# Attention and a mixture of experts on one core: four shared PSUM places, another order of a pair's jobs, the sums' guard on VectorE, own orders for the last pairs and the first expert block

## The chip, the core and the metric

The kernel runs on one core of a Trainium2 chip. The core has five engines with a queue each, worked off in order: TensorE (PE in the profile, with PEld for its weight loads), VectorE (DVE), ScalarE (ACT), GpSimd (POOL) and SyncE (SP, which here only issues DMAs). Matmul results go to PSUM, which is eight banks of 2 KB in each of 128 partitions; a tile of 128x512 fp32 numbers is one bank. The metric is the device time of one execution in microseconds (us), as the median of several runs.

## What is computed

Attention over 8 batches, 8 heads, 576 tokens of 64 numbers, and then a mixture of 8 experts, one for each token, over the 4608 rows that attention leaves.

```python
q_rot, k_rot = (rotate(q), rotate(k))
scores = scale * np.matmul(q_rot, k_rot.transpose(0, 1, 3, 2))
attn = np.exp(scores - np.max(scores, axis=-1, keepdims=True))
attn = attn / (np.sum(attn, axis=-1, keepdims=True) + 1e-09)
x = np.matmul(attn, v)            # to rows: 4608 x 512
logits = x @ w_gate + modality_bias[modality_id]
e_idx = np.argmax(logits, axis=1) # gate_w: the softmax at e_idx
h = np.maximum(x[mask] @ w1[e], 0.0)           # for each expert e
out[mask] = gate_w[mask, None] * (h @ w2[e])   # 512 -> 1024 -> 512
```

## The kernel before

**A pair's jobs.** Attention goes by 32 pairs of heads (`n`, four to a batch). Each pair is cut into named jobs, and each job is a call that puts its instructions on one engine:

- `T1`, `T2`, `R`, `HI`, `LO`, `SWH`, `SWL` rotate q and k two pairs ahead (POOL, and ACT for HI), split them into a high and a low part in a tile HL, and copy them by DMA to SW with the heads' halves of the partitions exchanged.
- `S0` to `S8` (`scores`, L314) are the scores of nine sets of 128 queries, six matmuls each (S8 twelve). `MN` (`rowmin`, L323, DVE) takes the extreme of a row, `EX` (`expo`, L330, ACT) the exponential with the row's sum.
- `F0` to `F3`, `FA`, `FB` (`fill`, L336, PE) transpose the exponentials into PSUM, 16 transposes to a full fill. `A_F` and `B_F` (`evac`) bring the two banks back to SBUF tiles PH and PD, one on ACT (L274), one on DVE (L368).
- `AVA` and `AVB` (`AV`, L392) multiply with V, `OTA` and `OTB` copy the result to SBUF (ACT), `OUT` (`outp`, L422) turns it and multiplies with the gate's weights, `EVA` and `EVB` (`ev`, DVE, three instructions each) divide by the row sums. For that `RE` (L406, ACT) adds 1e-9 to the sums and `RI` (L409, DVE) takes the reciprocal.
- Every fourth pair ends a batch: `XO` writes its rows to the DRAM tensor X, and fifteen steps of `route` on all engines, with five scatters `SC` (L532, POOL), put the batch's tokens into the experts' table TAB.

**PSUM.** S and F take the next of three places of two banks in turn (`RING`, `ring()`); AV, OUT and the routing's count take tiles of one bank from a pool of two (`psA`).

**The order.** No engine's order comes from a scheduler. Each job has a key (`KEYS`) in us; job x of pair n is sorted by `KEYS[x] + 14.438 * n`, and every engine gets its jobs in that order. A table `AT` has keys for the rest. Pairs 0, 1, 30 and 31 have some keys of their own.

**The experts.** The rows are worked through in blocks of 256 for one expert. A block (`s`) needs eight gathers of 128x128 numbers from X on POOL (`m_gather`, L795, 4 for each half of its rows) into one of two tiles XG (even blocks the one, odd blocks the other); DVE transposes both halves (`m_tr`, L840); ACT and DVE split them into XTH and XTL (`m_tre`). ACT and DVE split the weights into W1H, W1L, W2H and W2L (`m_hi`, `m_lo`). PE then runs four parts of the first layer (`l1.0` to `l1.3`, `m_l1`, L860, 24 matmuls each), ACT and DVE apply relu and split (`m_l1e`, L869 and L870), and PE runs the second layer for two halves of the rows (`m_l2`, L883, 24 matmuls each). ACT scales the result (L886), and POOL scatters it (L888).

The first block's work and the gathers of the first three blocks are jobs among the last pairs'. Block 1's gathers carry a wait for a matmul of block 0's first layer, the one that was last issued when the gather is written (`after`). From the second block on the code is a plain loop (`chain`), in whose order block 1's transposes and splits come first on DVE and ACT, ahead of block 0's results.

Of the kernel before, what the change touches and what calls it, by code (L numbers as in the profile page):

```python
# [8 lines left out]
F32 = mybir.dt.float32  # L9
# [36 lines left out]
AT = dict(
    rk=(23.0, 28.55, 31.2, 36.9, 41.45, 43.0, 44.4, 45.7, 54.6, 56.9, 57.4, 58.85, 60.2, 70.35, 73.3),
    bias=15.6,
    sc=(73.4, 87.85, 102.3, 116.7, 116.75),
    sce=(73.4, 73.45, 87.85, 87.9, 102.3),  # L50
    pl=(58.9, 70.4, 73.35, 84.85, 87.75, 99.3, 102.2, 113.7, 116.6),
    plan=(-49.7, -35.2, 6.0, 9.0),
    ix=(-41.5, -3.9, 6.1, 9.1),
    sine=-48.9,
    rows=(((0, -27.5, None), (1, -13.05, None), (2, -12.4, None), (3, -2.9, (30, "av", 0)), (5, 0.45, (30, "av", 1)),
           (7, 4.75, (30, "out", 1))), ((0, 11.15, ("l1", 0)),), ((0, 16.5, None),)),
    w1=(-21.6, -21.5, -16.2, -16.1),
    w2=(-9.9, -9.8, -9.7, -9.6),
    hi=(-14.8, -14.7, -0.4, -0.3),
    lo=(-11.8, -1.6, 10.8, 10.85),  # L60
    tr=(10.2, 10.21),
    te=(10.3, 10.4),
    hi2=(10.5, 10.98, 11.1, 11.2),
    lo2=(11.5, 11.55, 11.65, 11.75),
# [1141 lines left out]
```

## Time and profile before

| | us |
|---|---|
| median of 3 runs | 936.58 |
| lowest and highest | 933.55, 946.05 |
| the profiled execution's own time | 934.42 |
| its span from the first to the last instruction | 932.6 |
| granted TensorE clock over the span | 0.996 |

The profile gives one execution. Times in its views are us from the start of the span, durations of one instruction are in us in the timeline and in ns in the groups. A matmul's start is measured and its end modelled, so that overlapping matmuls count as busy also where they wait for each other. The pairs run from some 32 to 490 us, the expert blocks from 495 us to the end.

### The profile page before, as it was taken

What the parts mean: (1) busy time and instruction counts of PE and PEld (TensorE: products, weight loads), DVE (VectorE), ACT (ScalarE), POOL (GpSimd) and SP (SyncE); (2) the same over time, 40 slices, a digit from 0 to 9 for tenths busy, and PEclk for the clock granted to TensorE, in tenths of its full rate; (3) what the DMA queues carried; (4) which work ended last, traced back from release to release, by engine and by line L of the source; (5) the groups of instructions that cost most, each with busy time, mean ns of one, the idle gap of its engine ahead of it and who ended that gap; (6) DMA issues with size and microseconds to landing.
All of it is one profiled execution on the core that took longest, in us unless ns stands there. A gap on an engine that the chain in (4) does not pass through costs nothing.

```text
span 932.6 us, 24974 instructions
## 1 busy us (share of the span) xinstructions
PE 894.4 (96%) x9248; PEld 738.7 (79%) x9248; DVE 682.6 (73%) x1221; ACT 623.0 (67%) x1291; POOL 659.1 (71%) x494
## 2 busy tenths in 40 slices
PE   2999999999999999999999999999999999999996
PEld 2777777777777777777677888888888899789996
DVE  7678788877878778787886878766666666666663
ACT  3778787787877878778783655565555555455652
POOL 4988879889888988999833677566576665556410
PEclk9999999999999999999999999999999999999999
DMA  8865757678586885856752631127635112511240
GB/s 265 246 178 171 238 157 201 196 175 238 156 199 190 184 229 155 200 179 180 203 163 75 154 109 35 55 75 244 202 97 189 50 57 92 170 57 37 79 154 21
DMA packets 82301, 141.10 MB, mean 151 GB/s; under 512 B 28635, under 2 KB 52589, under 8 KB 81148
## 3 DMA queue, kind: packets, MB, share of 16 engines
q1 hardware_dynamic: 71660, 118.25, 44.9%
q0 software_dynamic: 9248, 19.46, 6.8%
q10 hardware_dynamic: 1264, 1.72, 0.6%
q8 instruction: 75, 1.23, 0.6%
q14 instruction: 54, 0.44, 0.2%
HBM read 140.33 MB, written 19.51 MB: 171 GB/s over the span
## 4 chain that ended last, share of the span: by engine, by line
PE 67%; ACT 16%; DVE 9%; issue 4%; another core or an unknown queue 1%; DMA 1%; POOL 0%; DVEq 0%; POOLq 0%; ACTq 0%
PE psH L860 22%; PE psY L883 21%; ACT P L330 13%; PE ps L314 10%; PE pa L392 9%; DVE mn L323 6%; PE ps L336 5%; ACT PH L274 2%; DMA SW<-HL 1%; DVE PH L368 1%; DMA ST<-in_qk_dram 1%; ACT HL L274 0%; ACT W2H L274 0%; DVE PD L368 0%
## 5 line engine op out<-in xcount | busy, mean ns | idle before, releaser
L330 ACT ACTIVATE P<-ps,mn 128x576 f32<-128x576 f32 x288 | 210.4, 737 | 94.1 <-DVE mn L323 94.1
L323 DVE TENSOR_REDUCE mn<-ps 128x1 f32<-128x576 f32 x288 | 204.1, 745 | 82.9 <-PE ps L314 37.3
L795 POOL DMA_INDIRECT XG<-X,iy x148 | 181.7, 1228 | 66.8 <-issue 50.2
L860 PE MATMUL psH<-HL,W1H 128*128 128x256 f32 x1152 | 202.6, 279 | 0.0
L314 PE MATMUL ps<-SW 64*128 64x288 f32 x960 | 166.4, 313 | 15.2 <-DMA SW<-HL 15.2
L860 PEld LDWEIGHTS psH<-HL,W1H 128*128 128x128 f32 x1152 | 176.8, 188 | 1.6
L314 PE MATMUL ps<-HL 64*128 64x288 f32 x960 | 165.9, 312 | 1.6 <-ACT P L330 1.5
L860 PE MATMUL psH<-HL,W1L 128*128 128x256 f32 x576 | 160.8, 279 | 0.2 <-DVE W1L L271 0.2
L314 PEld LDWEIGHTS ps<-HL 64*128 64x128 f32 x960 | 136.5, 189 | 23.5 <-issue 12.1
L314 PEld LDWEIGHTS ps<-SW 64*128 64x128 f32 x960 | 134.3, 189 | 26.2 <-DMA SW<-HL 13.5
L271 DVE TENSOR_TENSOR W1L<-ST,W1H 128x1024 fp32r<-128x1024 f32 x76 | 90.3, 1223 | 76.6 <-ACT W1H L274 68.8
L392 PE MATMUL pa<-PH,V 128*64 128x320 f32 (+1 forms) x1024 | 138.2, 412 | 0.0
L888 POOL DMA_INDIRECT out_dram<-y,ix x36 | 46.2, 1284 | 115.3 <-ACT y L886 69.7
L883 PE MATMUL psY<-W2H,SW 128*128 128x512 f32 (+1 forms) x304 | 118.8, 391 | 1.9 <-issue 1.5
L883 PE MATMUL psY<-W2L,SW 128*128 128x512 f32 (+1 forms) x304 | 119.7, 394 | 0.0
L336 PE MATMUL ps<-idf,P 64*128 64x64 f32 x2624 | 110.6, 229 | 9.5 <-ACT P L330 3.4
L336 PEld LDWEIGHTS ps<-idf,P 64*128 64x128 f32 x2624 | 93.2, 140 | 25.4 <-ACT PH L274 9.0
L291 POOL TENSOR_TENSOR HL<-ST,HL 128x1216 fp32r<-128x1216 f32 x31 | 85.9, 2772 | 33.1 <-ACT HL L274 33.1
L860 PEld LDWEIGHTS psH<-HL,W1L 128*128 128x128 f32 x576 | 108.3, 188 | 0.4 <-DVE W1L L271 0.4
L392 PEld LDWEIGHTS pa<-PH,V 128*64 128x64 f32 x1024 | 67.9, 136 | 48.4 <-issue 10.0
L368 DVE COPY PH<-ps 128x512 f32<-128x512 f32 (+1 forms) x160 | 96.0, 629 | 10.2 <-PE ps L336 9.3
L271 DVE TENSOR_TENSOR W2L<-ST,W2H 128x1024 fp32r<-128x1024 f32 x76 | 92.5, 1218 | 4.2 <-ACT W2H L274 3.6
(197 smaller groups left out, 1575.7 us busy)
## 6 DMA issues: line engine op xcount, KB each, us to landing
ST<-in_moe_w_dram SPq DMA_DIRECT2D x152, 512.0 KB
ST<-in_qk_dram SPq DMA_DIRECT2D x62, 608.0 KB
SW<-HL SPq DMA_DIRECT2D x124, 232.0 KB
V<-in_v_dram SPq DMA_DIRECT2D x32, 256.0 KB
X<-X SPq DMA_DIRECT2D x8, 1024.0 KB
XG<-X,iy POOLq DMA_INDIRECT x148
V<-in_v_dram SPq DMA_DIRECT2D x64, 16.0 KB
X<-XT SPq DMA_DIRECT2D x16, 64.0 KB
```

Of the source, the lines that this page charges most:

```text
L271: nc.vector.tensor_tensor(o, a, b, op=ALU.subtract)
L291: e.tensor_tensor(d["HL"][:, 1, c], a, d["HL"][:, 0, c].bitcast(F32), op=ALU.subtract)
L314: free(nc.tensor.matmul(ps[:, g, 0:288], t[:, wq, q0:q0 + P], t[:, wk, k0:k0 + 288], start=(m == 0), stop=(m == len(L) - 1)), seen)
L323: lastmin[d["ring", u]] = nc.vector.tensor_reduce(mn, d["S", u][:, :, 0:288], op=ALU.min, axis=AX.XY).ins
L330: nc.scalar.activation(p.rearrange("p (a b) -> p a b", a=2), ps[:, :, 0:288], AF.Exp, bias=d.pop(("m", u)), scale=-1.0, accum_out=d["sum"] ...
L336: free(nc.tensor.transpose(ps[0][:, g, c:c + 64], src[r, k0:k0 + P], idf[r, r]), ps[1])
L368: mine.append((nc.vector.tensor_copy if g else acopy)(o, i).ins)
L392: i = nc.tensor.matmul(pa[hh * 64:hh * 64 + 64, 0:c1 - c0], d["V"][:, hh, kt, :], r, start=(kt == 0), stop=(kt == 4))
L795: inst = nc.gpsimd.indirect_dma_start(out=XG[s % 2][:, t, g, :], out_offset=None, in_=X.rearrange("n (i f) -> (n i) f", f=P)[0:rows], in_o ...
L860: l1_[s] = nc.tensor.matmul(ps[:, i, :], w[:, c, f0:f0 + P], x[:, c, :], start=(m == 0), stop=(m == 11)).ins
L883: nc.tensor.matmul(ps, hx[:, c, t * P:(t + 1) * P], x[:, c, h * w:h * w + w], start=(m == 0), stop=(m == 23))
L888: inst = nc.gpsimd.indirect_dma_start(out=out.rearrange("n (i f) -> (n i) f", f=w) if nh > 1 else out, out_offset=bass.IndirectOffsetOnAxi ...
```

## The change

Four parts, in the words of the code:

1. The three places and the pool of two banks become four places of two banks, `SL`. A table `SLOTS` names the place of each job, and `take` and `give` keep account of idle banks; where the named place isn't idle at that point of the order, `take` chooses the one that has been idle longest. AV takes one bank of a place, OUT, S and F both.
2. `KEYS` has new values for a pair's jobs.
3. `RE` goes: the addition of 1e-9 is a `tensor_scalar` on DVE, right ahead of the reciprocal, in the job `RI`.
4. `EDGE` holds keys of their own for pairs 0, 1 and 25 to 31 (and for a load, some scatters and routing steps of pairs 3, 19 and 23), and `MOE` new keys for the first expert block and the gathers of the first three.

No matmul, exponential, evacuation, gather or scatter is added or taken away.

```diff
 KEYS = {
-    "S0": 0.00, "MN0": 1.75, "EX0": 3.14, "S1": -4.26, "MN1": -2.77, "EX1": -1.95, "S2": 3.22, "MN2": 3.92, "EX2":
...
+    "S0": 4.14, "MN0": 4.15, "EX0": 6.38, "S1": -0.75, "MN1": 0.49, "EX1": 0.96, "S2": -3.41, "MN2": -1.89, "EX2": 0.16, "S3": -6.54,
...
+SLOTS = {
+    "S0": 3, "S1": 2, "S2": 3, "S3": 2, "S4": 3, "S5": 0, "S6": 1, "S7": 0, "S8": 3, "F0": 0, "F1": 1, "F2": 0, "F3": 1, "FA": 1, "FB":
+    0, "AVA": 1, "AVB": 2, "OUT": 2, "RK8": 5, "L1": 0,
+}
...
-    rows=(((0, -27.5, None), (1, -13.05, None), (2, -12.4, None), (3, -2.9, (30, "av", 0)), (5, 0.45, (30, "av", 1)),
-           (7, 4.75, (30, "out", 1))), ((0, 11.15, ("l1", 0)),), ((0, 16.5, None),)),
...
+    rows=(-27.618, -3.472, -26.485, 5.591, 1.451, -0.002, -1.956, 6.898, 24.798, 24.558, 24.637, 20.800, 20.138, 18.320, 19.963, 20.651,
+        16.100, 20.637, 13.720, 17.155, 24.609, 20.570, 12.808, 24.437),
...
-    RING = [psS.tile([P, 2, 512], F32, name=f"ps{i}") for i in range(3)]
-    lastmin = [None] * 3
-    turn = [0]
-
-    def ring():
-        i = turn[0] % 3
-        turn[0] += 1
-        seen, lastmin[i] = lastmin[i], None
-        return i, RING[i], seen
+    SL = [psS.tile([P, 2, 512], F32, name=f"ps{i}") for i in range(4)]
+    lastmin = [[None] * 2 for _ in SL]
+    idle = {(i, b): i * 2 + b for i in range(4) for b in range(2)}
+    clock = [8]
+
+    def take(nm, bks):
+
+        own = SLOTS[nm]
...
+        if not all((own, b) in idle for b in bks):
...
+                own = min((i for i in range(4) if all((i, b) in idle for b in bks)), key=lambda i: max(idle[i, b] for b in bks))
+        seen = {}
+        for b in bks:
+            del idle[own, b]
+            seen[b], lastmin[own][b] = lastmin[own][b], None
+        return own, bks, seen
+
+    def give(own, *bks):
+        for b in bks:
+            idle[own, b] = clock[0]
+            clock[0] += 1
...
-    def rsum(n, part):
+    def rsum(n):
         d = st[n]
-        if part == 0:
-            d["re"] = sm.tile([P, 9], F32, name="re", tag="re")
-            nc.scalar.activation(d["re"], d["sum"], AF.Identity, bias=EPS)
-        else:
-            d["ri"] = sm.tile([P, 9], F32, name="ri", tag="ri")
-            nc.vector.reciprocal(d["ri"], d["re"])
+        d["re"] = sm.tile([P, 9], F32, name="re", tag="re")
+        nc.vector.tensor_scalar(d["re"], d["sum"], 1e-9, None, op0=ALU.add)
+        d["ri"] = sm.tile([P, 9], F32, name="ri", tag="ri")
+        nc.vector.reciprocal(d["ri"], d["re"])
...
-        po = [psA.tile([P, 512], F32, name="pa", tag="pa") for _ in range(2)]
+        own, _, seen = take("OUT", (0, 1))
+        po = [SL[own][:, h, :] for h in range(2)]
```

Three places in the order show what moves. Rows give the line, the operation, out<-in and the shape; a number behind x counts equal neighbours.

PE, one pair in the middle of attention, before: from OUT over the six fills to the first matmul of the next pair's S8 (`idf` marks a transpose, P_112 and P_122 to P_125 are the exponentials' tiles, ps the places).

```order
L422 MATMUL pa<-RW,oT_118 128x72 x10
L336 MATMUL ps_130<-idf,P_125 128x64 x16
L336 MATMUL ps_131<-idf,P_122 128x64 x16
L336 MATMUL ps_132<-idf,P_122 128x64 x2
L336 MATMUL ps_132<-idf,P_123 128x64 x2
L336 MATMUL ps_130<-idf,P_124 128x64 x16
L336 MATMUL ps_131<-idf,P_112 128x64 x10
L336 MATMUL ps_131<-idf,P_124 128x64 x2
L336 MATMUL ps_131<-idf,P_125 128x64 x2
L336 MATMUL ps_132<-idf,P_123 128x64 x16
L314 MATMUL ps_130<-HL_82 128x288
```

PE, the same stretch of the change: from the last matmul of the next pair's S8 over F3, FB and OUT to the first two of S6 (L405 is S, L428 a fill, L520 OUT).

```order
L405 MATMUL ps_130<-HL_82 128x288
L428 MATMUL ps_128<-idf,P_122 128x64 x16
L428 MATMUL ps_127<-idf,P_109 128x64 x10
L428 MATMUL ps_127<-idf,P_121 128x64 x2
L428 MATMUL ps_127<-idf,P_122 128x64 x2
L520 MATMUL ps_129<-RW,oT_115 128x72 x10
L405 MATMUL ps_128<-HL_82 128x288
L405 MATMUL ps_128<-SW_84 128x288
```

Before, a pair is S8 S1 S6, AVA, S7 S3 S0, AVB, S2 S5 S4, OUT, F3 F0 FA F2 FB F1; now it is S8, F3 FB, OUT, S6 S0 S5, AVB, FA, S4, F0 F1, S3 S7 S2, AVA, S1, F2. In the new order S0, F3, FB, FA, F0, F1, AVA and AVB are of one pair, OUT is of the pair before it, and the rest, with F2, of the pair behind it.

ACT, the same pair, before: three exponentials, then the six fills' evacuations in one stretch (PH and PD), then HI.

```order
L330 ACTIVATE P_123,sum<-ps_130,mn 128x576
L330 ACTIVATE P_124,sum<-ps_131,mn 128x576
L330 ACTIVATE P_124,sum<-ps_132,mn 128x576
L274 ACTIVATE PH<-ps_130 128x8x64
L274 ACTIVATE PH<-ps_131 128x8x64
L274 ACTIVATE PD<-ps_132 128x2x64
L274 ACTIVATE PH<-ps_130 128x8x64
L274 ACTIVATE PH<-ps_131 128x4x64
L274 ACTIVATE PD<-ps_131 64x64
L274 ACTIVATE PD<-ps_131 128x2x64
L274 ACTIVATE PH<-ps_132 128x8x64
L274 ACTIVATE HL_81<-ST_73 128x1216
```

ACT of the change, from F2's evacuation to the exponential behind HI (L421 is EX, L364 a copy).

```order
L364 ACTIVATE PH<-ps_127 128x8x64
L421 ACTIVATE P_119,sum<-ps_129,mn 128x576
L364 ACTIVATE PH<-ps_128 128x8x64
L421 ACTIVATE P_109,sum<-ps_130,mn 128x576
L364 ACTIVATE PH<-ps_127 128x4x64
L364 ACTIVATE PD<-ps_127 64x64
L364 ACTIVATE PD<-ps_127 128x2x64
L364 ACTIVATE HL_82<-ST_74 128x1216
L421 ACTIVATE P_122,sum<-ps_128,mn 128x576
```

The evacuations now stand between exponentials, one or two at a time.

POOL, behind the last pair, before: block 1's eight gathers (XG_76), block 0's first scatter, two scatters of batch 6 into TAB, and then block 2's eight gathers (XG_75).

```order
L795 DMA XG_76<-X,iy 128x128 x8
L888 DMA out_dram<-y,ix 4608x512
L521 CAST oi<-of 128x5
L450 COPY G<-BI 128x5x8
L532 DMA TAB<-VAL,oi 41472x2 x2
L787 TENSOR_SCALAR iy<-xi,CF 128x8
L795 DMA XG_75<-X,iy 128x128 x8
```

POOL of the change, from block 1's first gather (XG_76, L900) to its last; L638 scatters into TAB. Four of block 2's gathers (XG_75) stand just ahead of this piece.

```order
L900 DMA XG_76<-X,iy 128x128 x3
L900 DMA XG_75<-X,iy 128x128 x2
L900 DMA XG_76<-X,iy 128x128 x2
L638 DMA TAB<-VAL,oi 41472x2
L627 CAST oi<-of 128x5
L638 DMA TAB<-VAL,oi 41472x2
L900 DMA XG_75<-X,iy 128x128
L900 DMA XG_76<-X,iy 128x128
L900 DMA XG_75<-X,iy 128x128
L900 DMA XG_76<-X,iy 128x128
L638 DMA TAB<-VAL,oi 41472x2
L900 DMA XG_76<-X,iy 128x128
```

Block 1's last gather now has eleven gathers and three scatters ahead of it from block 1's first on; the first of these carries the wait for `l1.1`, since the first layer is now issued as l1.3, l1.0, l1.1, l1.2, with OUT of the last pair behind it and then the second layer.

More of the change, by code (lines that the diff above doesn't have):

```diff
@@ L387, in AV @@
         c0, c1 = (0, 256) if half == 0 else (256, 576)
-        pa = d["pa", half] = psA.tile([P, 512], F32, name="pa", tag="pa")
+        own, _, seen = take("AV" + "AB"[half], (half,))
+        pa = d["pa", half] = SL[own][:, half, :]
+        d["at", "av", half] = own
         for kt in range(5):
```

229 lines of the change are left out of this document (123 added, 106 removed), and 58 rows, old and new, of tables (EDGE, KEYS).

## The prediction

> **What bounds the kernel now.** First the page, then the stretches of the span, then who waits for whom, and last the timeline of one pair.
>
> ```profile
> PE 894.4 (96%) x9248; PEld 738.7 (79%) x9248; DVE 682.6 (73%) x1221; ACT 623.0 (67%) x1291; POOL 659.1 (71%) x494
> ```
>
> ```profile
> 240.00:360.00 120.00, 118.50 (x1662) 89.77 (x1660) 95.05 (x212) 95.62 (x252) 105.44 (x66) 1.00 0.74 192
> 480.00:500.00 20.00, 18.75 (x231) 13.80 (x228) 15.97 (x31) 16.39 (x34) 4.88 (x7) 1.00 0.07 16
> 500.00:520.00 20.00, 19.28 (x115) 16.25 (x116) 11.57 (x19) 6.63 (x10) 10.29 (x12) 1.00 0.30 91
> 600.00:700.00 100.00, 100.00 (x625) 89.29 (x624) 69.80 (x74) 58.30 (x72) 67.75 (x55) 1.00 0.47 148
> ```
>
> The columns of the stretches are length, then PE, PEld, DVE, ACT and POOL busy. PE is the bound in both halves: 118.5 of 120 us among the pairs, all of 100 us among the expert blocks. DVE, ACT and POOL have 25, 24 and 15 us of 120 free among the pairs. So PE's time is what the change can move: its waits, its changes from one kind of job to another, and the seam between pairs and blocks. What is lost at the seam isn't won back, since the blocks behind it leave PE no idle time.
>
> One pair, PE, from its first fill to the next pair's:
>
> ```profile
> 307.07 3.58 PE L336 MATMUL ps<-idf,P 64*128 64x64 f32 x82
> 310.59 0.37 PE L314 MATMUL ps<-HL 64*128 64x288 f32 x1
> ...
> 310.81 0.29 PE L314 MATMUL ps<-HL 64*128 64x288 f32 x1
> ...
> 312.44 0.29 PE L314 MATMUL ps<-SW 64*128 64x288 f32 x1
> 312.66 1.95 PE L392 MATMUL pa<-PH,V 128*64 128x256 f32 x16
> 314.44 0.60 PE L392 MATMUL pa<-PD,V 128*64 128x256 f32 x4
> 314.97 0.40 PE L314 MATMUL ps<-SW 64*128 64x288 f32 x1
> ...
> 315.21 0.29 PE L314 MATMUL ps<-SW 64*128 64x288 f32 x1
> ...
> 315.35 0.30 PE L314 MATMUL ps<-SW 64*128 64x288 f32 x1
> ...
> 316.37 2.38 PE L392 MATMUL pa<-PH,V 128*64 128x320 f32 x16
> ...
> 321.67 0.28 PE L336 MATMUL ps<-idf,P 64*128 64x64 f32 x2
> ```
>
> A pair takes 321.67 - 307.07 = 14.60 us. Two things in it aren't work. First, waits that count as busy:
>
> ```profile
> 307.79 0.71 PE L336 MATMUL ps<-idf,P 64*128 64x64 f32 x16
> 309.00 0.71 PE L336 MATMUL ps<-idf,P 64*128 64x64 f32 x16
> ```
>
> ```profile
> 307.63 0.74 ACT L330 ACTIVATE P<-ps,mn 128x576 f32<-128x576 f32 x1
> 308.26 0.20 ACT L330 ACTIVATION_READ_ACCUMULATOR P<-ps,mn 128x1 f32 x1
> 308.35 0.60 ACT L274 ACTIVATE PH<-ps 128x512 f32<-128x512 f32 x1
> ```
>
> A fill of 16 transposes takes 0.71, of which some 0.22 is the last one's length, so 0.033 from one to the next; 82 of them are 2.7 us, and the stretch takes 3.52 (307.07 to 310.59). 0.8 us are waits: FA for S4's exponential to end at 308.46, F2 at 309.00 for the evacuation of F3 that ends on ACT at 308.95. The scores behind it lose 0.2 more: 24 matmuls in 2.07 us (310.59 to 312.66), against 18 in 1.40 (314.97 to 316.37), which would be 1.87. Waits: 1.0 us a pair.
>
> Second, changes of kind. Within S, matmul pairs start 0.13 apart (315.21 to 315.35). From S to AVA it is 0.22 (312.44 to 312.66), 0.1 more. Into S the first pair takes 0.24 (314.97 to 315.21) or 0.22 (310.59 to 310.81), 0.1 more, and AV's last four matmuls and the gap take 0.53 (314.44 to 314.97) where four of AVA's twenty take 0.4, again 0.1. So 0.1 to 0.3, and I take 0.2 for each.
>
> **The change, part by part.** The profiled execution took 934.4 us; the median of the runs is 2.2 higher.
>
> *Order of a pair, and four places.* The order has 7 changes of kind a pair before and 12 now. Five more at 0.2 are 1.0 us. Against it, fills stand two at a time between scores, and a fourth place lets evacuations run under other matmuls, so the 1.0 us of waits goes if ACT and DVE keep pace, which their free time allows. Net 0 a pair. The ends: -0.5 if a change costs 0.1 and all waits go, +1.0 if it costs 0.3 and half of them stay; over the 24 pairs from 2 to 25, -12 and +24. I take 0, between a waiting that is measured and a price that is measured. What is late next if a wait goes is AVA, which needs F0, F1 and FA back on PH.
>
> The Trainium skill (TensorEngine Tiling (Array Packing), "Key Properties") says that a change of the tiling mode drains TensorE, and another tile of the same mode doesn't. The rows show 64*128 for scores and fills and 128*64 for AV alone, so by that rule the added changes would be free; the trace speaks against it at 310.59, where scores follow fills in the same mode and the first pair still takes 0.22. What the rule would make of the time is a rival below.
>
> *The sums' guard.* It leaves ACT and comes to DVE:
>
> ```profile
> L406 ACT ACTIVATE re<-sum,EPS 128x9 f32<-128x9 f32 x32 | 9.7, 303 | 0.0
> L409 DVE RECIPROCAL ri<-re 128x9 f32<-128x9 f32 x32 | 6.6, 206 | 0.3
> ```
>
> 32 times 0.30 us off ACT, about 32 times 0.21 on DVE (nearest row: the same 9 numbers). Both lie beside PE, in the 24 and 25 free us of 120 above: nothing. Without that cover it would be -0.1 to +0.2 a pair.
>
> *The start.* Pair 1's S8 starts when all of pair 0's fills are done:
>
> ```profile
> 30.31 0.74 ACT L330 ACTIVATE P<-ps,mn 128x576 f32<-128x576 f32 x1 [0.62 <-DVE mn L323]
> ```
>
> ```profile
> 32.16 0.38 PE L314 MATMUL ps<-HL 64*128 64x288 f32 x1
> ```
>
> Now S8 of pair 1 is ahead of five of the fills, in place 3, where pair 0's S8 was just before; it waits for that one's exponential, which ends some 0.85 us after 30.31, at 31.2. Behind it come 66 transposes at 0.033, 2.2 us, and a change: 33.6 against 32.16. I take +1.5 (0 to +3; the exponentials have fewer evacuations between them now, which could bring 30.31 forward).
>
> *Pairs 26 to 31.* Their own order replaces one in which weight splits and gathers cost time:
>
> ```profile
> 409.55 1.12 PE L336 MATMUL ps<-idf,P 64*128 64x64 f32 x22
> ```
>
> ```profile
> 485.89 0.28 PE L336 MATMUL ps<-idf,P 64*128 64x64 f32 x2 [0.28 <-ACT P L330]
> ```
>
> From pair 26's first fill to pair 31's it is 76.3 us, where five pairs of 14.60 are 73.0: 3.3 us to be had. I take -2 (-3.3 to +4; the weights' splits still stand between exponentials).
>
> *Block 0's second layer.* It starts at 508.57 and its last matmul at 521.07; block 1's took from 533.27 to 544.24:
>
> ```profile
> 508.57 0.40 PE L883 MATMUL psY<-W2H,SW 128*128 128x512 f32 x1
> ```
>
> ```profile
> 521.07 0.39 PE L883 MATMUL psY<-W2L,SW 128*128 128x512 f32 x1
> 521.30 0.39 PE L860 MATMUL psH<-HL,W1H 128*128 128x256 f32 x2
> ```
>
> ```profile
> 533.27 0.40 PE L883 MATMUL psY<-W2H,SW 128*128 128x512 f32 x1
> ...
> 544.24 0.40 PE L883 MATMUL psY<-W2L,SW 128*128 128x512 f32 x1
> ```
>
> 12.50 against 10.97, so 1.5 us were waits for the relu of the last parts. OUT now stands between l1.2 and the second layer and covers them: -1.5 (0 at worst).
>
> *Block 1's rows.* POOL, its eight gathers and two scatters:
>
> ```profile
> 499.19 1.05 POOL L795 DMA_INDIRECT XG<-X,iy  x1 [12.76 <-issue]
> ...
> 509.46 1.00 POOL L795 DMA_INDIRECT XG<-X,iy  x1 [0.30 <-issue]
> ...
> 519.78 1.01 POOL L532 DMA_INDIRECT TAB<-VAL,oi  x1 [0.17 <-POOL G L450]
> 521.10 1.63 POOL L532 DMA_INDIRECT TAB<-VAL,oi  x1 [0.30 <-issue]
> ```
>
> ```profile
> 498.16 0.28 PE L860 MATMUL ps<-HL,W1L 128*128 128x256 f32 x1
> 498.37 1.34 PE L422 MATMUL pa<-RW,oT 64*128 64x72 f32 x20
> 499.85 0.38 PE L860 MATMUL ps<-HL,W1H 128*128 128x256 f32 x1
> ```
>
> ```profile
> 514.29 1.29 DVE L840 STREAM_TRANSPOSE XG<-XG 128x512 f32<-128x512 f32 x2
> ```
>
> Gathers start 10.27 / 7 = 1.47 us apart, scatters 1.32, and the first starts 0.75 after l1.0's end (498.16 + 0.28). In the change let T be the end of l1.1, which the first gather waits for. Block 1's last gather starts at T + 0.75 + 11 x 1.47 + 3 x 1.32 + 0.2 = T + 21.1 and is issued at T + 22.1. Its landing has no row; before, it lay between 0 and 3.8 us (510.46 to 514.29, where nothing waited for it). I take 2, the middle: T + 24. The transposes come first on DVE's queue there, and ACT's splits wait behind them, ahead of the results of block 0 and of W1's split for block 1. Before, PE's block 1 started 7.0 us after the transposes (514.29 to 521.30) with PE busy to the end, so 7.0 is an upper bound; the two transposes alone take 1.29, and splits of the same tile follow them, so 3 is about the least. I take 6, nearer to what was run: T + 30.
>
> PE, meanwhile: l1.2 takes 24 x 0.117 = 2.8 (72 matmuls from 499.85 to 508.57 here), OUT 1.5 (498.37 to 499.85), the second layer 11.2 (533.27 to 544.24, and 0.2 for its last matmul). PE is free at T + 15.5. It waits 14.5 us for block 1's rows. The lower end has 3 in place of 6 and a landing of 0 in place of 2, 9.5; the upper has 7.0 and 3.8, some 17. Nothing hides it: DVE, ACT and PE's next matmuls all stand behind those rows, and block 2's rows, which were fetched instead, aren't wanted until a block later (521.30 to 544.24 and 0.2 is one, 23 us).
>
> The Trainium skill (DMA: Bandwidth & Descriptors, "Anatomy of one DMA — SWDGE (gpsimd) path") fits 2.0 us plus the bytes at 436 GB/s to such a transfer; for the 64 KB of a gather that is 2.15 us by my estimate, and the wait would be 14.7. No row here shows a landing by itself.
>
> **Sum.** 0 + 1.5 - 2 - 1.5 + 14.5 = +12.5: 946.9 against the profiled 934.4, and 949 against the median.
>
> **Rivals.**
> - *The rows come in time.* If gathers went faster where POOL doesn't share its time with DVE's splits, or if the order on POOL didn't bind: 949 - 14.5 = 934.5. The 1.47 pitch in a quiet stretch speaks against it. 0.10.
> - *Changes within one mode are free* (the skill's rule above). All five added changes are S, fills and OUT, so only the waits count: -1.0 a pair, -24, 925; with half the waits left 937. For it: the mode column. Against it: 310.59. 0.12.
> - *Slower by over 2%.* ACT gets fills and exponentials in turn, so an exponential that is late for a minimum holds up an evacuation, and PE with it. Place: S2 and S7, whose places were given up by an exponential or evacuation just before. It decides from +0.26 a pair ((955.3 - 949) / 24). At +0.4, which is two changes' worth, 959; at the end of the range above, 973. 0.17.
> - *Faster by over 2%.* It takes the first two together: 910. 0.05.
> - The forecast: 0.56, by itself 943 to 957.
>
> **Range and chances.** 2% (918 and 955.3) is about what a measurement of this kernel can tell from no change. The range 930 to 962 leaves out the last gains (0.05), half of the second rival (0.06) and the far end of the third (0.05). Slower: 0.15 of the third and 0.06 of the forecast, 0.21. Faster: 0.05 and 0.01 of the second, 0.06. Within 2%: 0.73.
>
> **What would show it.** In the profile after: a pair of 14.4 to 14.8 us, with PE's fills two at a time and no wait of F2 for ACT; scores of pair 1 some 1 to 2 us later; POOL's gathers of block 1 spread over 21 us with block 2's and scatters between them; DVE's first transpose of block 1 idle ahead of it for a DMA; and PE idle for some 14 us between block 0's second layer and block 1's first, which the page would show as a dip of PE near slice 23 of 40 (932.6 / 40 = 23.3 us each). Wrong would be: no such idle time, a pair under 14.0 or over 15.0, or the gathers' pitch under 1 us.

## The result and the profile after

| | us |
|---|---|
| changed kernel, median of 4 runs | 1006.44 (1002.53 to 1010.70) |
| kernel before, same chip | 936.68 |
| ratio | 1.0728 (1.0638 to 1.0818) |
| the profiled execution's own time, span | 1008.52, 1006.6 |

The change made the kernel 7% slower. The prediction had +12.5 us; the profiled span grew by 74.0, from 932.6. The page shows where to look, with its busy times, PE's slices and the granted clock (25.2 us a slice):

```profile
PE 917.5 (91%) x9248; PEld 760.6 (76%) x9248; DVE 721.2 (72%) x1253; ACT 623.3 (62%) x1259; POOL 663.5 (66%) x494
...
PE   2799998988898899989888949999999999999996
...
PEclk9999899897997997989999969999999999999999
```

and before (23.3 us a slice):

```profile
PE   2999999999999999999999999999999999999996
...
PEclk9999999999999999999999999999999999999999
```

PE has the same 9248 matmuls and is busy 23.1 us longer (917.5 against 894.4), while the row of the clock, all nines before, dips six times in attention (the 5th, 8th, 10th, 13th, 16th and 18th digit). DVE has 32 instructions more, which the prediction put at 0.21 us each, 6.7 in all, and is busy 38.6 us longer. The one deep dip of PE (4, the 24th digit) is the seam between blocks 0 and 1.

The stretches, with the columns as before (length, then PE, PEld, DVE, ACT and POOL busy, clock, share of the DMA engines, GB/s):

```profile
240.00:360.00 120.00, 109.46 (x1425) 83.83 (x1425) 90.92 (x188) 80.53 (x207) 88.96 (x56) 0.91 0.62 164
580.00:600.00 20.00, 6.22 (x26) 4.98 (x25) 7.65 (x13) 7.55 (x12) 10.29 (x9) 0.65 0.31 47
600.00:700.00 100.00, 100.00 (x659) 91.18 (x658) 75.99 (x132) 57.91 (x72) 69.90 (x56) 0.99 0.31 86
```

Among the pairs PE did 1425 matmuls in 120 us where it had done 1662. The blocks behind the seam are as full as before.

The waits of PE (total, times, longest), of which the wait of 12.4 and one of 2.9 for SW are at the start of the kernel:

```profile
PE ps L405 <- DMA SW<-HL: 33.1, 16, 12.4
...
PE psH L964 <- ACT W1H L364: 13.2, 1, 13.2
```

So 18 us of waits for SW stand in attention, where the prediction had none. These waits are for the copies by SWH and SWL that bring the heads' halves of HL to the other partitions.

To compare kernels I cut each span at starts of matmuls: at pair 2's first matmul of S8 (A), pair 26's (B), and the start of the last matmul of block 0's second layer (C); D is the time from the first matmul of block 0's second layer to that of block 1's, E the same from block 1's to block 2's. Later blocks take 22.4, but for a stray wait in some kernels.

| kernel | start to A | A to B | B to C | D | E | span |
|---|---|---|---|---|---|---|
| before | 46.8 | 351.7 | 122.6 | 24.7 | 22.4 | 932.6 |
| changed | 50.1 | 393.4 | 139.3 | 39.7 | 22.4 | 1006.6 |

The 74.0 us are +3.3 at the start, +41.7 over pairs 2 to 25, +16.7 from pair 26 to C, and +12.3 behind it: D is 15.0 longer, block 0's second layer is itself 1.4 shorter, which D's start doesn't show, and the kernel before once lost some 3.8 us at 807 to 813 by a wait and a low clock, which the changed one didn't.

### The profile page after: what moved, and what is told of

Read it like the earlier page. It is cut to its first block, busy times and chain, and to the rows that moved or that the text cites. A ratio compares the mean times of both kernels' runs of the same rounds, so it can differ in the third digit from the quotient of the medians.

```text
span 1006.6 us, 24867 instructions
## 1 busy us (share of the span) xinstructions
PE 917.5 (91%) x9248; PEld 760.6 (76%) x9248; DVE 721.2 (72%) x1253; ACT 623.3 (62%) x1259; POOL 663.5 (66%) x494
## 3 DMA queue, kind: packets, MB, share of 16 engines
q0 software_dynamic: 9248, 19.46, 6.6%
q10 hardware_dynamic: 1264, 1.72, 0.5%
## 5 line engine op out<-in xcount | busy, mean ns | idle before, releaser
L421 ACT ACTIVATE P<-ps,mn 128x576 f32<-128x576 f32 x288 | 210.8, 737 | 66.0 <-DVE mn L414 63.8
L405 PE MATMUL ps<-SW 64*128 64x288 f32 x960 | 190.6, 330 | 41.0 <-DMA SW<-HL 33.1
L900 POOL DMA_INDIRECT XG<-X,iy x148 | 179.8, 1215 | 67.9 <-issue 44.9
L964 PE MATMUL psH<-HL,W1H 128*128 128x256 f32 x1152 | 205.1, 281 | 13.2 <-ACT W1H L364 13.2
L405 PE MATMUL ps<-HL 64*128 64x288 f32 x960 | 196.2, 331 | 10.8 <-ACT P L421 9.3
L405 PEld LDWEIGHTS ps<-SW 64*128 64x128 f32 x960 | 144.7, 202 | 62.0 <-DMA SW<-HL 33.9
L964 PEld LDWEIGHTS psH<-HL,W1H 128*128 128x128 f32 x1152 | 178.7, 190 | 15.1 <-ACT W1H L364 13.6
L405 PEld LDWEIGHTS ps<-HL 64*128 64x128 f32 x960 | 147.0, 201 | 17.8 <-ACT P L421 12.1
L488 PE MATMUL ps<-PH,V 128*64 128x256 f32 (+1 forms) x1024 | 143.8, 424 | 9.6 <-DVE PH L462 7.0
L428 PEld LDWEIGHTS ps<-idf,P 64*128 64x128 f32 x2624 | 105.8, 145 | 27.0 <-ACT P L421 18.1
L428 PE MATMUL ps<-idf,P 64*128 64x64 f32 x2624 | 115.8, 232 | 5.2 <-DVE PH L462 2.6
L488 PEld LDWEIGHTS ps<-PH,V 128*64 128x64 f32 x1024 | 71.2, 141 | 61.1 <-issue 11.1
L364 ACT ACTIVATE PH<-ps 128x512 f32<-128x512 f32 (+1 forms) x160 | 88.2, 557 | 44.6 <-PE ps L428 33.6
```

Source lines behind the costliest of these rows:

```text
L364: return nc.scalar.activation(o, i, AF.Copy, scale=scale)
L405: free(nc.tensor.matmul(ps[:, g, 0:288], t[:, wq, q0:q0 + P], t[:, wk, k0:k0 + 288], start=(m == 0), stop=(m == len(L) - 1)), seen[g])
L421: nc.scalar.activation(p.rearrange("p (a b) -> p a b", a=2), ps[:, :, 0:288], AF.Exp, bias=d.pop(("m", u)), scale=-1.0, accum_out=d["sum"] ...
L428: free(nc.tensor.transpose(ps[0][:, g, c:c + 64], src[r, k0:k0 + P], idf[r, r]), ps[1][g])
L488: i = nc.tensor.matmul(pa[hh * 64:hh * 64 + 64, 0:c1 - c0], d["V"][:, hh, kt, :], r, start=(kt == 0), stop=(kt == 4))
L900: inst = nc.gpsimd.indirect_dma_start(out=XG[s % 2][:, t, g, :], out_offset=None, in_=X.rearrange("n (i f) -> (n i) f", f=P)[0:rows], in_o ...
```

## Three theories, and the pair in which they part

Pairs 2 to 26 of the changed kernel are of three sorts. Most take 14.1 to 14.5 us, where they took 14.6; I call them undisturbed. Pairs 11, 15, 19 and 23, beside which a batch is routed, take 16.6, where they took 14.8. And the third pair behind a batch's last takes 19.6 to 22.8 (6, 10, 14, 18 and 22), or 27.2 (26, whose next pair has an order of its own). The timeline of PE, pairs 2 and 10 from the first matmul of their S8 to the next pair's, and what stands in the second:

```profile
50.11 0.38 PE L405 MATMUL ps<-HL 64*128 64x288 f32 x1
...
64.21 0.40 PE L405 MATMUL ps<-HL 64*128 64x288 f32 x1
...
169.95 0.40 PE L405 MATMUL ps<-HL 64*128 64x288 f32 x1
...
171.74 0.40 PE L405 MATMUL ps<-SW 64*128 64x288 f32 x1 [1.40 <-DMA SW<-HL]
...
173.56 0.60 PE L405 MATMUL ps<-SW 64*128 64x288 f32 x1 [1.42 <-DMA SW<-HL]
...
192.58 0.40 PE L405 MATMUL ps<-HL 64*128 64x288 f32 x1
```

The waits make 2.8 us, but the pair is 22.63 - 14.10 = 8.5 us longer than pair 2. The rest is in the clock, the third number from the right of each stretch:

```profile
170.00:172.00 2.00, 0.60 (x3) 0.32 (x3) 1.15 (x2) 1.42 (x4) 2.00 (x1) 1.00 0.97 221
172.00:174.00 2.00, 0.58 (x6) 0.44 (x6) 0.00 (x0) 0.00 (x0) 0.25 (x1) 0.71 0.97 348
174.00:182.00 8.00, 8.00 (x81) 7.31 (x81) 5.35 (x11) 3.59 (x8) 0.45 (x1) 0.50 0.23 86
182.00:184.00 2.00, 2.00 (x14) 0.91 (x12) 0.00 (x0) 1.64 (x6) 2.00 (x1) 0.73 0.68 151
```

The clock fell during the second wait and stayed at 0.50 for 8 us in which PE was busy throughout: 1.16 + 8 + 1.08 = 10.2 us at half speed, which lose 5.1. With the waits that is 7.9 of the 8.5. The DMA share of 0.97 in the first two windows says what else was moving. SP's queue, ahead of it:

```profile
163.15 0.33 SPq L543 DMA_DIRECT2D X<-X  x1
163.58 2.12 SPq L545 DMA_DIRECT2D X<-XT  x2
165.79 3.27 SPq L389 DMA_DIRECT2D SW<-HL  x4
169.11 0.58 SPq L266 DMA_DIRECT2D ST<-in_qk_dram  x1
```

and the same place in the kernel before, where half of the copies are out ahead of X:

```profile
151.05 1.29 SPq L299 DMA_DIRECT2D SW<-HL  x2
152.43 0.54 SPq L443 DMA_DIRECT2D X<-X  x1
153.02 2.31 SPq L445 DMA_DIRECT2D X<-XT  x2
155.42 2.21 SPq L299 DMA_DIRECT2D SW<-HL  x2
```

**Theory 1, SP's order.** `XO`, the write of a batch's rows (1024 KB in its one large transfer), waits for the batch's last EVB and now stands on SP ahead of the four copies (232 KB each) of a pair three further on, while that pair's S8, their first reader, has moved 8.8 us forward. By the keys, the write stood at 27.00 - 3 x 14.438 = -16.3 of that pair before, behind SWH (-17.41) and ahead of SWL (-11.79), with S8 at -5.22; now it stands at -19.4, ahead of SWH (-18.86) and SWL (-18.48), with S8 at -14.04. Rival: the write is harmless, and the copies are late by themselves because S8 moved.

**Theory 2, the guard.** DVE's `tensor_scalar` on 9 numbers is not short. The group (count, then least, median and longest ns) and two places on DVE and POOL:

```profile
L503 DVE TENSOR_SCALAR re<-sum x32: 153/1192/1710, 46.4 to 572.2; 128x9 f32<-128x9 f32 x32
```

```profile
165.40 1.32 DVE L503 TENSOR_SCALAR re<-sum 128x9 f32<-128x9 f32 x1
166.75 0.22 DVE L505 RECIPROCAL ri<-re 128x9 f32<-128x9 f32 x1
```

```profile
163.90 2.78 POOL L373 TENSOR_TENSOR ST<-ST,ST 128x1216 f32<-128x1216 f32 x1
```

It ends at 166.72, just after POOL's operation at 166.68; the reciprocal behind it, with the next POOL operation running, takes its usual 0.22. Of the 32, 27 take over 0.2 us, and each of these ends 0.03 or 0.04 us after a `tensor_tensor` of the rotation on POOL; of the five that take 0.15 or 0.16, none does. Rival: DVE has 25 us of 120 free, so a microsecond a pair costs nothing.

**Theory 3, the seam.** Block 1's gathers, spread behind block 2's and the scatters, are what D's 15 us are. Rival: something else in that block binds as soon as they are early.

## The experiments

Every ratio is to the kernel before on the same chip, with its 95% interval. Its medians there lay between 934.35 and 938.89, so a difference of a few us between kernels of different sets shows nothing by itself. All but b3, b4 and d3 start from the changed kernel.

### One part each, and the three together

**a1**, the write of X behind the copies:

```diff
-"XO": 23.88
+"XO": 25.20
```

> One key of the changed kernel: XO (a batch's rows to X) goes from 23.88 to 25.20, so that on SP's queue the copies SWH and SWL of the pair three behind stand ahead of it. Theory 1 (SP's order makes SW late in every fourth pair, and PE's wait for it brings the half clock): the waits of PE for SW go, the granted clock stays at 1.00 among the pairs, and pairs 6, 10, 14, 18, 22 and 26 take some 14.3 us in place of 19.6 to 27.2: about 46 us less, 960. Rival A (the half clock comes by itself, whatever PE waits for): only the waits go, some 3 us a time: 988. Rival B (SW is late since HL's low part is late on ACT and POOL): no change, 1006.

977.45 us, 1.0461 (1.0424 to 1.0497): 29.0 less than the changed kernel. The waits for SW and the half clock left the pairs, up to pair 26 (the row of the clock):

```profile
PEclk9999999999999999989999879999999999999999
```

The slow pairs went to 15.1 and 16.35, not to 14.3, and pair 26 stayed near where it was (25.9). So the gain is less than the expected 46: SP's next transfer is now late, V's load behind the write, with its worst wait in pair 26:

```profile
423.84 4.54 PE L488 MATMUL ps<-PH,V 128*64 128x320 f32 x16 [4.73 <-DMA V<-in_v_dram]
```

**a2**, the guard back on ACT, ahead of the reciprocal by 0.6 in the order:

```diff
-nc.vector.tensor_scalar(d["re"], d["sum"], 1e-9, None, op0=ALU.add)
+nc.scalar.activation(d["re"], d["sum"], AF.Identity, bias=EPS)   # job RE, key RI - 0.6
```

> The changed kernel with the sums' guard back on ACT, 0.6 us ahead of the reciprocal in the order. Theory 2 (on DVE the guard's tensor_scalar waits until the operation that POOL runs is over, median 1.19 us in place of 0.15): DVE's busy time falls by some 38 us to about 683, and the four pairs 11, 15, 19 and 23, 16.6 us now, take some 14.3: 9 us less, 997. Rival A (the delay is hidden beside PE everywhere): 1006. Rival B (it costs in every pair): 15 us or more, under 992.

987.86 us, 1.056 (1.0519 to 1.0602): 18.6 less. On ACT it takes 0.29 and never more than 0.32:

```profile
L503 ACT ACTIVATE re<-sum,EPS x32: 291/294/317, 45.1 to 549.2; 128x9 f32<-128x9 f32 x32
```

Pairs 2 to 5, at 14.1 to 14.5, went to 13.93, pairs 11, 15, 19 and 23 from 16.6 to 15.5 to 15.9. Rival A (hidden by DVE's free time) is out, and it is rival B, a cost in every pair, that came true; theory 2's own size of 9 us was half of it.

**a3**, block 1's rows next to each other ahead of block 2's and the scatters:

```diff
-24.798, 24.558, 24.637, 20.800, 20.138, 18.320, 19.963, 20.651,   # block 1
-16.100, 20.637, 13.720, 17.155, 24.609, 20.570, 12.808, 24.437,   # block 2
+18.301, 18.302, ... 18.308
+24.801, 24.802, ... 24.808
```

> The changed kernel with the eight gathers of block 1 in one run on POOL, ahead of block 2's and of the scatters that stood between. Theory 3 (block 1's rows come late since other work stands between them): the last gather is issued some 11 us behind the first in place of 19.7, PE's wait ahead of block 1 falls from 13 us to about 4, and the half clock there (to 603 us) goes as well: 9 and 3 us, 994. Rival (the landing or the wait for the splits of W1 sets it): no change, 1006.

1004.58 us, 1.0723 (1.0656 to 1.079): next to nothing. PE's wait at block 1's first matmul did fall, from 13.2 to 3.4, but D became 42.8: block 1's first layer now took 27.9 us (584.40 to 612.33), with the clock at 0.50 from 584.20 to 608.09 and PE pausing again and again. ACT waited in its queue in front of block 0's second result, and two of W1's splits stand behind that; whether PE's pauses are for them, the profile doesn't say:

```profile
597.70 0.69 ACT L990 ACTIVATE y<-psY,ix 128x512 f32<-128x512 f32 x1 [12.40 <-remote]
```

So theory 3 names a cause that is there but doesn't stand alone.

**a4**, the three together:

> All three edits together. If the three costs are separate they add: 46, 9 and 12 us less, 939. If one wait hides behind another, 945 to 960. What is left against the kernel before is then in pairs 26 to 31 and at the start.

964.55 us, 1.0327 (1.0262 to 1.0391): 41.9 less, where the three alone sum to 29.0 + 18.6 + 1.9 = 49.5. The difference lies in the five slow pairs 6 to 22. There a1 takes 29.3 us off, a2 7.2, a3, which changes nothing there, 5.1, and the three together 33.1. So part of it is overlap, and part scatter from run to run.

### Each suspect in the kernel before

**b4**, `XO` ahead of both copies, and nothing else:

```diff
-"XO": 27.00
+"XO": 25.52
```

> The kernel before with XO ahead of SWH on SP (25.52 in place of 27.00), as in the changed kernel. Theory 1 in full (it takes both, the write ahead of SW and the scores of S8 some 9 us earlier in their pair): S8 waits for SW by under 1 us in every fourth pair, no half clock, 934 to 940. Rival (the place of XO on SP does it alone): six waits of 2 to 5 us with half clock behind them, 960 or more.

937.3 us, 0.998 (0.9935 to 1.0026). The write's place costs nothing by itself; S8 is late enough in its pair there. So theory 1 needs both of its halves, the write ahead of the copies and S8 moved forward.

**b3**, the guard on DVE, and nothing else:

```diff
-nc.scalar.activation(d["re"], d["sum"], AF.Identity, bias=EPS)
+nc.vector.tensor_scalar(d["re"], d["sum"], 1e-9, None, op0=ALU.add)
```

> The kernel before with one part of the change alone: the guard as a tensor_scalar on DVE, ahead of the reciprocal. Theory 2 (it waits there for POOL's operation): median of the guard over 1 us, DVE's busy time up by 25 to 40 us, and 4 to 10 us slower, 942. Rival A (in this order what stands behind it on DVE isn't urgent): DVE busier, the time the same, 934 to 936. Rival B (the delay comes from the new order, not from DVE and POOL): 0.2 us each, 934.

960.25 us, 1.024 (1.0182 to 1.0298). In the order of before it costs more, since there it stood ahead of minima that exponentials, and PE, wait for:

```profile
L406 DVE TENSOR_SCALAR re<-sum x32: 130/1726/3001, 39.4 to 518.2; 128x9 f32<-128x9 f32 x32
```

```profile
PE ps L314 <- ACT P L330: 23.6, 20, 2.0
```

**d3** asks whether another instruction would do, with an SBUF tile of 1e-9 as second operand:

```diff
+nc.vector.tensor_tensor(d["re"], d["sum"], EPS.to_broadcast([P, 9]), op=ALU.add)
```

> The kernel before with the guard on DVE, as a tensor_tensor with a tile of the constant in place of the tensor_scalar. The reciprocal of the same 9 numbers never took over 0.22 us beside POOL's operations, so not every operation waits. If only the form of tensor_scalar waits: 0.2 us each, 935 to 938. If an operation with two inputs in SBUF waits too: a median over 1 us and 950 or more, like the 960 of the tensor_scalar.

```profile
L406 DVE TENSOR_TENSOR re<-sum,EPS x32: 127/1735/3118, 39.5 to 519.2; 128x9 f32<-128x9 f32 x32
```

962.89 us, 1.0275 (1.0215 to 1.0334): the same. The Trainium skill (SBUF — State Buffer, "Who interferes with whom") says that DVE and GpSimd share a pair of SBUF ports as an exclusive lock, which `tensor_scalar` can take in its two-port modes and which a `tensor_tensor` with both inputs in SBUF wants against GpSimd's reads, and that the other then blocks for a whole instruction. The two groups agree with it: an operation that takes 0.13 at best has a median length of 1.73, and in each group the 21 longest, all over 0.4 us, end 0.02 to 0.04 us after a `tensor_tensor` of the rotation on POOL. No run here shows the ports themselves.

### Mending the order on SP

**b1**: a4 with V's load ahead of the write, the write later still, the guard on ACT right behind the last exponential, block 2's rows behind block 0's first result:

```diff
-"LV": 4.14, "XO": 23.88
+"LV": -16.50, "XO": 27.20      # LV of pairs 26 to 31 to -16.4 and -12.2 too
```

> The three edits together, and three more: V's load goes from 4.14 to -16.50 and XO to 27.20, so that V too stands ahead of a batch's rows on SP (in pairs 26 to 31 as well); the guard on ACT stands right behind its pair's last exponential; block 2's gathers stand behind the first scatter of block 0's results on POOL. Theory 1 goes on: what was left of every fourth pair (some 1.4 us) was V behind the 1 MB write, and the 5.2 us and the half clock in pair 26 as well: no wait of PE for SW or V, the clock at 1.00 to the end of the pairs, 16 us less than with the three edits. Theory 3: ACT's 12 us of waiting ahead of the second y go: some 4 us less. Together about 945. Rival (the write of X, later now, holds up the next batch's rows): 960 and waits of DVE for it.

989.33 us, 1.0538 (1.0439 to 1.0638). The rival of this step hit: with the write that late, DVE's next writes to its source wait for it (up to 5.8 us), and PE waits for DVE. Of what it is slower than a4, only 6.6 us stand in pairs 2 to 25; 17.9 stand from B to C, where PE also waits 3.7 and 4.3 us for SW.

**b2**: b1 without the own orders of pairs 23 and 25 to 31:

> The kernel of b1 with the steady order of a pair for pairs 25 to 31, in place of their own. Theory 4 (the own order of the last pairs costs, since it puts evacuations and fills where their inputs are late): the stretch from pair 26's to pair 31's S8 goes from about 82 us to 73 to 76, some 8 us less than b1. Rival (that stretch is lost to weight splits and gathers whatever the order): the same as b1, or slower.

971.47 us, 1.035 (1.0287 to 1.0413), 17.9 less than b1. From pair 26's S8 to pair 31's it takes 90.8, not the expected 73 to 76 (b1 106.4, the changed kernel 92.3), and from B to C 150.3, where the changed kernel takes 139.3. So the general order is no cure for the last pairs.

**c1**: copies, then X, then V early, then q and k:

```diff
-"LV": 4.14, "XO": 23.88
+"LV": -16.50, "XO": 25.20      # LV of pair 26 to -16.4; guard, rows as b1
```

> XO back to 25.20, and V's load at -16.50 right behind it, ahead of the loads of q and k; in pairs 27 to 31 V stays where the change puts it. The guard on ACT behind the last exponential, block 1's gathers in one run, block 2's behind the first scatter of results. Theory 1: no wait of DVE for X (up to 5.8 us with XO at 27.20), none of PE for V or SW up to pair 26 but under 1 us a time, clock at 1.00: pairs at 13.85, those of the routing at 15.5, the stretch from pair 2's S8 to pair 26's some 341 us, and together about 940. Rival (a megabyte of writes and V's load slow each other wherever they stand): waits of 1.4 us in every fourth pair stay, 350 us for that stretch, 950.

957.15 us, 1.0178 (1.0093 to 1.0263). Pairs 2 to 25 take 344.2, 7.5 less than in the kernel before and 3 more than expected; most of the 17 us above the expected 940 stand behind them. A pair of 13.84, and the stretch that the prediction began with (1688 matmuls, clock 1.00):

```profile
63.95 0.38 PE L405 MATMUL ps<-HL 64*128 64x288 f32 x1
...
77.79 0.38 PE L405 MATMUL ps<-HL 64*128 64x288 f32 x1
```

```profile
240.00:360.00 120.00, 115.54 (x1688) 89.30 (x1684) 96.38 (x215) 99.09 (x256) 106.29 (x64) 1.00 0.68 194
```

### The seam and the last pairs

**c2** is c1 with block 1's rows at 13.30 to 13.31, and **c3** the changed kernel with those rows and block 2's at 25.15 to 25.16 alone:

> The same, with block 1's gathers in the order right behind the first part of block 0's first layer that is issued (l1.3), in place of the third (l1.1): they start some 5.6 us earlier. Theory 3 (block 1 waits for its rows and what hangs on them): the time from block 0's second layer to block 1's falls from some 30 to 35 us to about 26, 5 to 8 us less than the kernel without it. Rival (it is the reports of PE to ACT, or W1's splits, that are late there): no change.

> The changed kernel with nothing but the order of POOL's gathers altered: block 1's behind the first part of block 0's first layer, block 2's behind the first scatter of results. Theory 3: the time from block 0's second layer to block 1's, 39.7 us in the changed kernel and 24.7 before, falls to 25 to 28, so 12 to 15 us less, 993. Rival, as with the gathers alone put together (42.8 us there): the wait only moves to W1's splits, 1003 or more.

957.38 us, 1.0222 (1.0144 to 1.03), and 1007.89, 1.0736 (1.0652 to 1.0819). In both D is back (25.1 and 24.8, before 24.7), and both give it away again. In c3, POOL's gathers stand ahead of routing steps that DVE needs, and PE waits for the first layer's result:

```profile
571.93 0.20 DVE L624 TENSOR_REDUCE of<-rk 128x5 f32<-128x40 f32 x1 [7.73 <-issue]
```

```profile
575.64 0.79 PE L987 MATMUL psY<-W2H,SW 128*128 128x512 f32 x1 [6.60 <-DVE HX L974]
```

B to C is 7.3 longer (146.6 against 139.3), and block 2's rows, now late, make E 30.3 in place of 22.4. In all five kernels with block 2's rows at that place (b1, b2, c1, c2, c3) E is 29.9 to 31.0, in the others that start from the changed kernel 22.4 to 23.2.

**d1** is c1 with both blocks' rows behind the routing and ahead of the results, and without a load of q and k that pair 29's own order pulls ahead:

```diff
-"LD": -47.730                     # pair 29
+rows 15.421 ... 15.428, 15.431 ... 15.438
```

> As c1 (XO, V, guard on ACT), and pair 29's load of q and k back at its steady place, so that it no longer stands ahead of pair 27's SW on SP; the gathers of blocks 1 and 2 stand behind the routing step that DVE waits for, and in one run each. Theory 1: the 3.7 us that pair 27's S5 waits for SW at 411 us and the half clock behind it go, 6 us. Theory 3: no wait for HX ahead of the second layer (6.6 us in c2), blocks 0 and 1 at 25 to 28 us each in place of 25 and 30: 8 to 10 us less than c2. Together 940 to 944. Rival (something else keeps SW late there, such as the registers that SP loads): 950.

952.13 us, 1.015 (1.0093 to 1.0208). E is 22.4 again and D 27.0. B to C went from 139.6 to 132.2; 4.0 of that stand from pair 26's S8 to pair 27's, where the load was moved, and 3.3 behind pair 31's S8, where the gathers were. The wait in pair 27 that the loads on SP made, in c2 (3.64 in c1) and here:

```profile
410.96 0.40 PE L405 MATMUL ps<-SW 64*128 64x288 f32 x1 [3.81 <-DMA SW<-HL]
```

```profile
417.85 0.40 PE L405 MATMUL ps<-SW 64*128 64x288 f32 x1 [1.30 <-DMA SW<-HL]
```

Pairs 2 to 25 took 8.8 longer than in c1, with stray waits and low clock in pairs 13, 15, 16 and 21, whose cause stays open. So it missed the expected 940 to 944.

**d2** is d1 with the reciprocal taken of the sums themselves; it leaves out the addition of 1e-9.

> d1 with the guard left out: the reciprocal is taken of the sums themselves. If the 1.7 us that the pairs with routing take more than the others (15.65 against 13.85 to 14.2) come from the reciprocal waiting for the guard on ACT, they fall to 14.3 or so, and four of them make 5 us; ACT is freed of 32 times 0.3 us. 5 us less than d1. Rival (they come from the routing's own operations): the same as d1.

954.66 us: two runs at 942.53 and 948.70 and two at 960.61 and 967.35, too scattered for a ratio. Of the pairs with routing, 11 takes 15.90 as in d1, and 19 and 23 take 15.0 against 15.6 (in 15, d1 has a stray wait). So at most 0.6 of the 1.8 to 2.1 us by which they lie above 13.84 is the guard's; the rest stays open. Its D was 35.9 with the same order on POOL as d1's 27.0.

All spans, by the cuts defined above:

| kernel | start to A | A to B | B to C | D | E | span |
|---|---|---|---|---|---|---|
| a1 write later | 51.5 | 363.2 | 137.5 | 40.1 | 22.4 | 976.6 |
| a2 guard on ACT | 50.0 | 376.2 | 137.9 | 40.2 | 22.4 | 988.7 |
| a3 rows together | 49.2 | 389.7 | 141.7 | 42.8 | 22.4 | 1007.9 |
| a4 all three | 51.0 | 350.5 | 139.0 | 34.6 | 23.2 | 961.0 |
| b1 V early, write late | 48.3 | 357.1 | 156.9 | 29.9 | 31.0 | 985.6 |
| b2 without own orders | 49.0 | 355.5 | 150.3 | 25.3 | 30.9 | 972.7 |
| b3 before, guard on DVE | 47.8 | 375.8 | 123.1 | 24.7 | 22.4 | 959.6 |
| b4 before, write early | 46.3 | 352.8 | 122.5 | 24.7 | 25.5 | 939.2 |
| c1 copies, X, V | 50.1 | 344.2 | 139.6 | 29.8 | 29.9 | 956.1 |
| c2 and rows first | 47.7 | 344.9 | 143.6 | 25.1 | 30.3 | 951.3 |
| c3 rows alone | 49.8 | 392.3 | 146.6 | 24.8 | 30.3 | 1004.2 |
| d1 loads and rows | 48.9 | 353.0 | 132.2 | 27.0 | 22.4 | 952.9 |
| d2 without guard | 48.2 | 343.0 | 132.6 | 35.9 | 22.5 | 946.9 |
| d3 before, tensor_tensor | 47.9 | 376.8 | 122.8 | 24.5 | 22.4 | 956.7 |

b4's E, its next block (26.8) and d1's block behind E (26.5) hold stray waits, as the kernel before has one at 807.

No kernel is faster than the one before. The nearest with the new order and the whole computation, d1 and c1, are 1.5% and 1.8% slower, though c1's pairs are faster.

## Why the prediction was wrong, step by step

- **The order of a pair and the places** (predicted net 0, -0.5 to +1.0 a pair). For what it priced, PE's own waits and changes of kind, it was a little too dear: undisturbed pairs take 14.1 to 14.5 in the changed kernel, 13.93 with the guard on ACT and 13.84 in c1, against 14.60. If all of the 1.0 us of waits went, five more changes cost 13.84 - 13.60 = 0.24, some 0.05 each and not 0.2; how much of the waits went was not measured. The rival by which changes within one mode are free was the nearer of the two, and the 0.1 read at 310.59 was the start of a group and not a price paid by the whole pair.
- **What failed first** is the sentence behind it: "What is late next if a wait goes is AVA." It asked only PE, DVE and ACT. S8 moved some 9 us forward, its operands come over SP's queue, and nothing on that queue (XO, SWH, SWL, LV, LD) was priced, although the keys of all of them are in the table that changed. That is +30.2 of the +41.7 us over pairs 2 to 25 by a1. The third rival forecast a slower kernel by late exponentials at S2 and S7, and so had the sign for another reason.
- **What failed second** is the term for the clock, which the sum lacks. A wait was priced at its length. Five such events among pairs 2 to 25, each with 2 to 3 us of waits for SW, cost 39 us there against pairs of 14.10 (19.61 + 22.63 + 22.15 + 22.77 + 22.69, less 5 x 14.10), more of it by half speed than by waiting.
- **The sums' guard** (predicted nothing, -0.1 to +0.2 a pair). The count was right and the size of one instruction wrong: 1.19 us in the median and not 0.21, because the nearest row, a reciprocal of the same nine numbers, never waits for POOL and this one does. It cost 17.2 us over pairs 2 to 25 by a2, 0.72 a pair, and 18.6 in all. "Both lie beside PE, in the free us" was also wrong: DVE's free time is spread through the pair, and a queue in order makes what stands behind it late.
- **The start** (predicted pair 1's S8 at 33.6) came at 33.90, from 32.16. Right; by pair 2 it is 3.3.
- **The last pairs** (predicted -2, at worst +4). B to C grew by 16.7, of which block 0's second layer, measured below, took 1.4 off. One part is the same wait for SW with a half clock behind it, in pair 26 (2.56 us at 446.80, clock low to 456). Another is SP's loads pulled ahead, by d1 some 4 us against c1. What remains in d1, 132.2 against 122.6, some 9.6 us, was not taken apart.
- **Block 0's second layer** (predicted -1.5): 571.74 to 582.80, 11.07 against 12.50, so -1.4. Right.
- **Block 1's rows** (predicted a wait of 14.5 us). Right in mechanism, as c3 shows, where earlier rows bring D back to 24.8, and near in size. T, the end of l1.1, is 567.46. POOL's first and last gather, DVE's transposes and PE's block:

```profile
568.21 1.07 POOL L900 DMA_INDIRECT XG<-X,iy  x1 [0.34 <-POOL iy L892]
...
586.88 1.02 POOL L900 DMA_INDIRECT XG<-X,iy  x1 [0.30 <-issue]
```

```profile
591.62 1.30 DVE L945 STREAM_TRANSPOSE XG<-XG 128x512 f32<-128x512 f32 x2 [16.14 <-DMA XG<-X,iy]
```

```profile
582.80 0.40 PE L987 MATMUL psY<-W2L,SW 128*128 128x512 f32 x1
...
596.39 0.79 PE L964 MATMUL psH<-HL,W1H 128*128 128x256 f32 x2 [13.19 <-ACT W1H L364]
```

The first gather at T + 0.75, as predicted; the last at T + 19.4 (21.1), the transposes at T + 24.2 (24), PE's block at T + 28.9 (30), PE free at T + 15.6 (15.5). The size is partly luck: the gathers came quicker than the 1.47 apart that were taken (1.7 less in all), the last landing took 3.7 and not 2, and from the transposes to PE it was 4.8 and not 6. D is 15.0 longer by the wait of 13.2, some 3.3 for the half clock that goes on for 6.55 us behind it, and 1.4 less for the second layer. What the step didn't see is that other things stand close behind: with the gathers early, routing or block 2's rows bind (c3), or block 1's first layer goes slowly (a3), and of these orders only d1's gets most of it back without paying for it in E.

The sum had 12.5. Its terms for the start, the second layer and the seam, 1.5 - 1.5 + 14.5, came near; it had 0 where pairs 2 to 25 grew by 41.7, and -2 - 1.5 where the stretch from B to C, second layer included, grew by 16.7.

## What to carry to other kernels

When jobs are moved, walk through every queue that they are moved past, the one that only issues transfers included: ask of each moved reader when its transfer is issued, behind which larger one, and what that one waits for. Price a wait of TensorE with the low clock that can follow it, which in pair 10 cost nearly twice the wait (5.1 for 2.8): it came in steps of 3.41 us, and each step that is full of work loses 1.7. A small operation that leaves one engine for another is priced by a row of its own kind beside the same neighbours, not by a row of the same size; the guard belongs on ACT here.

## What the runs showed of the hardware

**The clock goes by steps of 3.41 us, and one half-idle step halves it.** In the changed kernel the low clock starts at 111.41, 172.85, 241.12, 309.39, 377.65 and 445.92, and all of these lie 18 or 20 times 3.41 us apart. Among the pairs it lasts 6.83 or 10.24, two or three steps, and in b3 3.41, one. So the length of a wait doesn't decide alone. In b3, one of 1.77 halved the clock and one of 1.78 didn't:

```profile
243.22 0.40 PE L314 MATMUL ps<-HL 64*128 64x288 f32 x1 [1.77 <-ACT P L330]
...
369.19 0.40 PE L314 MATMUL ps<-HL 64*128 64x288 f32 x1 [1.78 <-ACT P L330]
```

The step in which each of them ends, and the step behind it:

```profile
241.58:244.99 3.41, 1.77 (x34) 1.77 (x36) 2.91 (x6) 2.65 (x8) 3.41 (x2) 1.00 0.37 123
244.99:248.41 3.42, 3.42 (x69) 3.38 (x67) 2.91 (x7) 2.63 (x6) 1.98 (x1) 0.50 0.71 182
...
367.87:371.28 3.41, 2.09 (x44) 2.09 (x46) 2.92 (x6) 2.98 (x8) 3.41 (x2) 1.00 0.31 73
371.28:374.70 3.42, 3.05 (x82) 2.94 (x78) 3.29 (x11) 3.04 (x10) 1.65 (x1) 1.00 0.61 176
```

The first wait lies almost wholly in one step, which leaves PE 1.77 us of work there; the second began in the step before. The other two falls of b3 come behind steps with 1.40 and 1.62 us of work, and 1.83 was enough to keep the clock at 1.00. The border isn't that sharp everywhere: in d1 a step with 1.72 kept it and one with 1.94 didn't. In the changed kernel two waits of 1.4 in pair 10 left 1.29 us of work in the step ahead of the fall; in a1, where no wait from 50 to 420 us is over 1.44, the clock never fell there. The Trainium skill (TensorE: Matmul & The Clock Gate, "What's actually happening") gives one idle window of about 3.4 us before the clock falls and 3.4 us of sustained work before it returns. The length of the step agrees, but PE was busy for 1.29 to 1.94 us of the steps ahead of these falls, and in pair 10 the clock stayed at 0.50 for one more step behind 3.41 us of full work; the measurements decide.

**The same order, two seams.** D was 27.0 in d1 and 35.9 in d2, with the same order of gathers. In a3 many of PE's instructions at 588 to 602 stand 0.7 to 1.5 us apart, with "issue" as what they waited for, and ACT's wait of 12.40 for the second layer's result ends at 597.70, 17 us after PE's last matmul of it is shown to start (580.60). Why that stretch varies stays open.
